# The output projection of half the heads, with 512 columns a matmul and one column of weights

## Chip, cores and metric

The kernel runs on one core of a Trainium2 chip. The metric is the device time of one execution in microseconds (us); the median of several executions is compared.

## What is computed

Two attention layers, A and B, decode one token each, with the same sizes: model width 512, 32 heads of 128, a cache of 8192 keys and values per head, bf16. The two results of 512 numbers are put side by side.

```python
def _A_ref(x, k_cache, v_cache, wq, wo):        # B is the same
    q = (x @ wq) as 32 heads of 128
    scores = jnp.einsum("bhqd,bhkd->bhqk", q, k_cache) * (Dh ** -0.5)
    p = _softmax(scores, axis=-1)
    o = jnp.einsum("bhqk,bhkd->bhqd", p, v_cache)
    return o.reshape(1, 1, 32 * 128) @ wo
...
return jnp.concatenate([a, b], axis=-1)
```

The caches are 256 MiB of the 285 MB that are read; each byte is used once.

## The kernel before

**Tiling.** The 64 heads go in 16 rounds `n` of four (A is rounds 0 to 7, B is 8 to 15). In a round, 32 partitions hold one head, with 256 keys (T) in each partition. `kn` has two buffers for K, `vn` one for V.

**One round.** SyncE (SP) loads K of the next round and V of this one. VectorE (DVE) multiplies K with q in four parts (`plan_mul`, L337). TensorE (PE) folds the 128 products of a key to 8 with identity matmuls of 512 columns (`plan_red`, L346), DVE adds those (`plan_sr`, L357). The maximum is found (`plan_max`, `plan_gmax`: L363, L369, L372) and broadcast with four fp32 matmuls of one row of weights (`plan_exp`, L382); ScalarE (ACT) writes the exponentials to `pt`. In the next round, between its third and fourth fold, PE adds up the sums (`plan_sum`, L399) and multiplies with V in 256 matmuls of four columns (`plan_pv`, L415), and DVE divides (`plan_o`, L424) into `oD`, one column per head, head dimension on partitions.

**wo.** `wo` lies in the K buffer that comes free first (`wo_sb`). A's is loaded whole, B's in pieces of 16, 8, 4, 2, 1 and 1 heads (`WOG`). For a piece of n heads a partition holds n whole rows of wo, one after the other, so `oD` has to be laid out again for pieces of more than one head: `plan_relayout` takes a product with a mask on DVE (L453), a matmul with a selector on PE (L458), and a copy on DVE into `o2` (L462). `plan_wo` (L473) then has wo as weights, 128x128, and one column of `o2` as the moving operand: four matmuls for each of the piece's `j`, which add up in four columns of the bank `qyp`, output columns on partitions. `plan_y` (L481) copies the four columns to `yT`, `plan_out` transposes the eight columns of A and B with one matmul (L485), copies (L488) and stores them with one DMA.

**Order.** Each engine runs a list of instructions written out by hand, in the order in which the plan calls them; a wait stands before the instruction that needs it. All loads are on SP's queue, in order: K of round 15, then A's wo and B's first 16 heads, V of the last round in two pieces (`VLAST`, 192 and 64 of the 256), then the small pieces of B's wo. PE runs rounds 1 to 15 in a loop. The work that follows the last round's scores, A's wo and B's first 16 heads and the layout of B's next two pieces, is a block that PE branches to after round 15 (`cuts[NM][0]` to `[1]`), then it returns to the loop's code for the last `plan_sum` and `plan_pv`, and after that it branches to the last block, with the small pieces and the output. In the program's code the last block stands ahead of the other.

`hrow` [1, 4, 128] fp32 is the constant that `plan_exp` broadcasts with. `rps` has two banks that `plan_red` writes by turns.

Of the kernel before, what the change touches and what calls it, by code (L numbers as in the profile page):

```python
# [8 lines left out]
BF16 = mybir.dt.bfloat16  # L9
F32 = mybir.dt.float32  # L10

P = 128
# [11 lines left out]
class _Plan:  # L24
# [6 lines left out]
    def wait(self, eng, mark):  # L31
        if mark is None:
            return
        ctr, val = mark
        if val <= 0 or self.waited.get((eng, ctr.name), 0) >= val:
            return
        self.waited[(eng, ctr.name)] = val
        self.prog[eng].append((None, ctr, val))

    def op(self, eng, fn, ctr=None, needs=(), inc=1):  # L40

        for m in needs:
            self.wait(eng, m)
        self.prog[eng].append((fn, ctr, inc))
        if ctr is None:
            return None
        ctr.n += inc
        return ctr, ctr.n
# [81 lines left out]
def bass_concat_heads__mha_block_cached__gqa_block_cached__decode_kernel(  # L130
# [18 lines left out]
    NA = 2  # L149
    H, Sk, Dh = ks[0].shape[1:]  # L150
    D = xs[0].shape[2]
    NOUT = wos[0].shape[1]
# [9 lines left out]
    NM = NA * QA  # L162
    NK = 2
    CT = 64
    NCH = T // CT
# [3 lines left out]
    WOG = [[(0, 32)], [(0, 16), (16, 8), (24, 4), (28, 2), (30, 1), (31, 1)]]  # L169
# [4 lines left out]
    with ExitStack() as st:  # L174
# [3 lines left out]
        def sb(name, shape, dt):  # L178
            return ec(nc.sbuf_tensor(name, shape, dt))
# [4 lines left out]
        def flat(ap):  # L184
            return ap.rearrange("p t d -> p (t d)")
# [6 lines left out]
        wo_sb = [flat(kn[:, KW])[:, a * W:(a + 1) * W].rearrange("p (j n) -> p j n", n=NOUT)  # L192
                 for a in range(NA)]
# [6 lines left out]
        ones_f = sb("ones_f", [P, P], F32)  # L200
        ident = sb("ident", [P, P], BF16)
        ident_f = sb("ident_f", [P, P], F32)
        hrow = sb("hrow", [1, G, P], F32)
# [5 lines left out]
        oD = sb("oD", [P, NA, H], BF16)  # L209
        zb = sb("zb", [P, 2, P], BF16)  # L210
        o2 = sb("o2", [P, NA, H], BF16)
        mask = {g: sb("mask%d" % g, [P, P // g], BF16) for g in RG}
        jsel = {g: sb("jsel%d" % g, [P, g], BF16) for g in RG}
        NQ = NOUT // P
        yT = sb("yT", [P, NA, NQ], BF16)
        out_q = sb("out_q", [NA * NQ, P], BF16)

        def ps(name, shape):
            return ec(nc.psum_tensor(name, shape, F32))

        rps = ps("rps", [P, 2, 512])
        acc = ps("acc", [P, 512])
        mtp = ps("mtp", [P, 512])
        bmp = ps("bmp", [P, 512])
        misc = ps("misc", [P, 512])
        qyp = ps("qyp", [P, 512])

        pl = _Plan()
        op, wait = pl.op, pl.wait

        def ctr(name):
            return _Ctr(nc, st, name)
# [6 lines left out]
        s_out = ctr("s_out")  # L239
        c_pool, c_dve, c_act, c_pe = ctr("c_pool"), ctr("c_dve"), ctr("c_act"), ctr("c_pe")  # L240
        c_mul, c_red, c_sr, c_pv = ctr("c_mul"), ctr("c_red"), ctr("c_sr"), ctr("c_pv")

        def dma(eng, dst, src, c, needs=()):
            return op(eng, lambda e: e.dma_start(dst, src), c, needs, inc=16)  # L244


        def const(fn, needs=()):
# [5 lines left out]
            out=ident[:], in_=ones_bf[:], pattern=[[1, P]], compare_op=ALU.is_equal,  # L253
            fill=0.0, base=0, channel_multiplier=-1), [i_onesb])
        i_identf = const(lambda e: e.affine_select(
            out=ident_f[:], in_=ones_f[:], pattern=[[1, P]], compare_op=ALU.is_equal,
# [9 lines left out]
        k_in, v_in, wq_in, wo_in = {}, {}, {}, {}  # L266
        red_done, pv_done, q_done, wo_done = {}, {}, {}, {}
# [25 lines left out]
        for a in range(NA):  # L293
# [6 lines left out]
            m = op("PE", xmm, c_pe, [x_in, i_onesb])  # L300
            x_ready = op("ACT", lambda e, a=a: e.copy(
                xb[:, a].rearrange("p c m -> p (c m)"), (misc if a == 0 else qyp)[:]), c_act, [m])
        misc_free, qy_free = [x_ready], [x_ready]
# [25 lines left out]
        mul_done, sr_done, p_done, m_done, r_done, o_done = {}, {}, {}, {}, {}, {}  # L329
        turn = [None]  # L330

        def nth(n, m=1):
            return slice(n * m, (n + 1) * m) if turn[0] is None else bass.ds((turn[0] * NK + n) * m, m)
# [42 lines left out]
        nb_done = {}  # L376
# [46 lines left out]
        def plan_o(n):  # L423
            o_done[n] = op("DVE", lambda e: e.tensor_tensor(  # L424
                oD[:].rearrange("p a h -> p (a h)")[:, nth(n, G)], acc[:, 0:G],
                rinv[:, nth(n), :].rearrange("p o g -> p (o g)"), ALU.mult),
                c_dve, [pv_done[n], r_done[n]])
# [14 lines left out]
        o2_ready = {}  # L442

        def plan_relayout(*groups):
            assert len(groups) <= 2
            made = []
            for a, g in groups:
                h0, n = WOG[a][g]
                z = z_n[0] % 2
                z_n[0] += 1  # L450
                s = P // n
                zv = zb[:, z, :].rearrange("p (h s) -> p h s", s=s)
                made.append((a, g, h0, n, z, op("DVE", lambda e, a=a, h0=h0, n=n, s=s, zv=zv: e.tensor_tensor(  # L453
                    zv, oD[:, a, h0:h0 + n].unsqueeze(2).broadcast_to([P, n, s]),
                    mask[n][:, None, :].broadcast_to([P, n, s]), ALU.mult),
                    c_dve, [sel_ready[n], o_done[a * QA + (h0 + n - 1) // G], z_free.get(z)])))
            for a, g, h0, n, z, m in made:
                z_free[z] = op("PE", lambda e, n=n, z=z: e.matmul(  # L458
                    z_ps[z][:, 0:n], zb[:, z, :], jsel[n][:], start=True, stop=True),
                    c_pe, [m, z_read[z][0]])  # L460
            for a, g, h0, n, z, m in made:
                o2_ready[a, g] = z_read[z][0] = op("DVE", lambda e, a=a, h0=h0, n=n, z=z: e.tensor_copy(  # L462
                    o2[:, a, h0:h0 + n], z_ps[z][:, 0:n]), c_dve, [z_free[z]])

        def plan_wo(a, g):

            h0, n = WOG[a][g]

            def mm(e):
                r = None  # L470
                for j in range(h0, h0 + n):
                    for i in range(NQ):
                        r = e.matmul(qyp[:, i:i + 1], wo_sb[a][:, j, i * P:(i + 1) * P],  # L473
                                     (o2 if n > 1 else oD)[:, a, j:j + 1], start=(j == 0 and i == 0),
                                     stop=(j == H - 1 and i == NQ - 1), skip_group_check=True)
                return r
            wo_done[a] = op("PE", mm, c_pe, [o2_ready[a, g] if n > 1 else o_done[a * QA + h0 // G],
                                            wo_in[a, g], qy_free[0]])

        def plan_y(a):  # L480
            qy_free[0] = op("DVE", lambda e: e.tensor_copy(yT[:, a, :], qyp[:, 0:NQ]), c_dve,  # L481
                            [wo_done[a]])

        def plan_out():
            m = op("PE", lambda e: e.matmul(bmp[0:NA * NQ, 0:P], yT[:].rearrange("p a q -> p (a q)"),  # L485
                                            ident[:], start=True, stop=True),
                   c_pe, [qy_free[0], nb_done[NM - 1]])
            m = op("DVE", lambda e: e.tensor_copy(out_q[:], bmp[0:NA * NQ, 0:P]), c_dve, [m])  # L488
            done = dma("SP", out[0].rearrange("o (q n) -> (o q) n", q=NA * NQ), out_q[:], s_out, [m])
            wait("SP", done)  # L490


# [50 lines left out]
            load_wo(1, g)  # L543
        z_read[1][0] = gm_done[NM - 1]
        plan_relayout((0, 0), (1, 0))
        plan_wo(0, 0)
        plan_y(0)
        plan_wo(1, 0)
        plan_relayout(*[(1, g) for g in early[BEFORE:]])
        wait("PE", misc_free[0])  # L550
        cuts[NM].append(len(pl.prog["PE"]))
# [2 lines left out]
            plan_pv(NM - 1, t0, t1)  # L554
        cuts[NM].append(len(pl.prog["PE"]))
        plan_o(NM - 1)
        plan_wo(1, BEFORE)
        plan_relayout(*[(1, g) for g in range(len(early), NB) if WOG[1][g][1] > 1])
        for g in range(BEFORE + 1, NB):
            plan_wo(1, g)  # L560
        plan_y(1)
        plan_out()

        for name, at in (("SP", block.sync), ("PE", block.tensor), ("ACT", block.scalar),
# [76 lines left out]
```

## Time and profile before

| | |
|---|---|
| median of 3 runs | 667.73 us (667.52 to 667.88) |
| profiled execution | 668.01 us, of which the span from first to last instruction is 666.28 us |
| mean granted clock of TensorE | 0.756 |
| busy share of the span | PE 66%, DVE 51%, ACT 9%, POOL 0% |
| DMA | 285 MB, 428 GB/s over the span |

Times inside the span are counted from its start. PE is a matmul, PEld the load of its weights, and the two overlap. Matmuls are pipelined, so that the duration of one (165 ns for one of a single column) is not the distance to the next. A granted clock of 1.00 is full, 0.50 half. "issue" marks idle time in which the engine waited for nothing that the profile shows.

### The profile page before, as it was taken

The page shows a single profiled execution, that of the slowest core. Times are in us where ns is not written, and L with a number is a line of the kernel's source. Part 1 is how long each engine was busy: PE and PEld are TensorE (multiplying, and loading weights), DVE is VectorE, ACT ScalarE, POOL GpSimd, SP SyncE. Part 2 cuts the span into 40 slices and gives each one's busy share as a digit, 9 for nine tenths or more (in the row PEclk, how much of TensorE's full clock was granted, in tenths as well). Part 3 has the DMA queues.
Part 4 walks back from the last instruction along what each step waited for, and adds up shares of the span by engine and source line. Part 5 has one row for each costly group of instructions (what it writes and reads, how often), then busy time and mean ns, then how long its engine had stood idle before and what let it go on. Part 6 is the DMA issues. An engine that isn't in the chain of part 4 may idle for free.

```text
span 666.3 us, 12449 instructions
## 1 busy us (share of the span) xinstructions
PE 440.7 (66%) x5646; PEld 252.4 (38%) x5646; DVE 340.2 (51%) x215; ACT 62.4 (9%) x151; POOL 2.8 (0%) x15
## 2 busy tenths in 40 slices
PE   2065875938487594848658484865948486685866
PEld 1022352615244261614425161442626144252645
DVE  1095818356381835638083563809256481925610
ACT  1002002020201002020200202020020202002020
POOL 1000000000000000000000000000000000000000
PEclk9678777769787775978777587877658797765875
DMA  9999999999999999999999999999999999999996
GB/s 378 437 445 438 438 431 433 409 437 441 441 429 433 441 441 425 417 437 441 441 421 441 441 433 429 417 441 441 441 421 441 437 433 429 421 441 441 407 454 274
DMA packets 6076, 285.33 MB, mean 428 GB/s; under 512 B 690, under 2 KB 948, under 8 KB 1204
## 3 DMA queue, kind: packets, MB, share of 16 engines
q1 hardware_dynamic: 6064, 285.22, 99.2%
q8 instruction: 6, 0.10, 0.1%
q14 instruction: 2, 0.02, 0.0%
q10 hardware_dynamic: 4, 0.00, 0.0%
HBM read 285.21 MB, written 0.00 MB: 428 GB/s over the span
## 4 chain that ended last, share of the span: by engine, by line
DMA 62%; PE 25%; DVE 10%; issue 2%; SPq 0%; DVEq 0%; another core or an unknown queue 0%; ACT 0%
DMA kn<-in_B_k_cache_dram 21%; DMA kn<-in_A_k_cache_dram 19%; PE rps L346 15%; DMA vn<-in_A_v_cache_dram 14%; PE acc L415 10%; DVE kn L337 9%; DMA vn<-in_B_v_cache_dram 5%; DMA kn<-in_B_wo_dram 4%; SPq L244 0%; DVE s_sb L357 0%; PE qyp L315 0%; DVEq L117 0%; PE misc L399 0%; ACT qbc L323 0%
## 5 line engine op out<-in xcount | busy, mean ns | idle before, releaser
L346 PE MATMUL rps<-kn,ident 128*128 128x512 bf16 x1024 | 294.5, 456 | 171.7 <-DVE kn L337 171.7
L337 DVE TENSOR_TENSOR kn<-kn,qbc 128x8192 bf16<-128x8192 bf16 x64 | 281.5, 4419 | 98.5 <-DMA kn<-in_A_k_cache_dram 59.0
L346 PEld LDWEIGHTS rps<-kn,ident 128*128 128x128 bf16 x1024 | 112.5, 114 | 340.6 <-issue 266.3
L415 PE MATMUL acc<-pt,vn 128*128 128x4 bf16 x4096 | 108.8, 165 | 5.6 <-DMA vn<-in_B_v_cache_dram 2.4
L415 PEld LDWEIGHTS acc<-pt,vn 128*128 128x128 bf16 x4096 | 108.3, 100 | 6.2 <-DMA vn<-in_B_v_cache_dram 2.7
L357 DVE TENSOR_REDUCE s_sb<-rps 128x64 f32<-128x512 f32 x64 | 44.0, 688 | 110.9 <-PE rps L346 110.9
L394 ACT ACTIVATE pt<-s_sb,negb 32x256 bf16<-32x256 f32 x64 | 54.8, 857 | 2.1 <-ACT negb L386 0.2
L386 ACT ACTIVATE negb<-bmp 128x1 f32<-128x1 f32 x16 | 2.7, 171 | 528.8 <-PE bmp L382 528.8
L424 DVE TENSOR_TENSOR oD<-acc,rinv 128x4 f32 (+1 forms) x16 | 2.6, 163 | 90.9 <-PE acc L415 90.9
L382 PE MATMUL bmp<-gm,hrow 1*128 1x1 f32 x128 | 17.0, 249 | 6.0 <-DVE gm L372 6.0
L382 PEld LDWEIGHTS bmp<-gm,hrow 1*128 1x128 f32 x128 | 15.6, 188 | 10.7 <-DVE gm L372 10.0
L369 PE MATMUL mtp<-ident_f,m 128*1 128x128 f32 x32 | 6.1, 271 | 19.8 <-DVE m L363 19.8
L394 ACT ACTIVATION_READ_ACCUMULATOR pt<-s_sb,negb 32x1 f32 x64 | 15.9, 248 | 0.0
L369 PEld LDWEIGHTS mtp<-ident_f,m 128*1 128x1 f32 x32 | 1.4, 81 | 27.7 <-DVE m L363 27.7
L473 PE MATMUL qyp<-o,kn 128*128 128x1 bf16 x248 | 7.4, 165 | 4.9 <-issue 3.5
L315 PE MATMUL qyp<-vn,xb 128*32 128x512 bf16 x64 | 5.9, 496 | 5.8 <-DMA vn<-in_A_wq_dram 4.3
L473 PEld LDWEIGHTS qyp<-o,kn 128*128 128x128 bf16 x248 | 7.0, 102 | 5.4 <-issue 3.9
L372 DVE TENSOR_REDUCE gm<-mtp 1x4 f32<-1x128 f32 x16 | 4.5, 279 | 7.6 <-PE mtp L369 7.6
L399 PEld LDWEIGHTS misc<-rsum,ones_f 128*128 128x128 f32 x32 | 6.2, 197 | 3.5 <-issue 1.4
L363 DVE TENSOR_REDUCE m<-s_sb 128x1 f32<-128x256 f32 x16 | 6.7, 420 | 0.5
L323 ACT CAST qbc<-qyp 128x512 bf16<-128x512 f32 x4 | 2.3, 586 | 43.0 <-PE qyp L315 43.0
L297 PE MATMUL misc<-ones_bf,kn 1*128 1x128 bf16 x4 | 0.6, 302 | 8.0 <-DMA kn<-in_B_x_dram 8.0
(36 smaller groups left out, 25.1 us busy)
## 6 DMA issues: line engine op xcount, KB each, us to landing
vn<-in_B_v_cache_dram SPq DMA_DIRECT2D x1, 6144.0 KB, 22.2
vn<-in_A_wq_dram SPq DMA_DIRECT2D x1, 4096.0 KB, 12.4
vn<-in_B_wq_dram SPq DMA_DIRECT2D x1, 4096.0 KB, 40.6
kn<-in_A_wo_dram SPq DMA_DIRECT2D x1, 4096.0 KB, 35.1
kn<-in_B_wo_dram SPq DMA_DIRECT2D x1, 2048.0 KB, 39.6
vn<-in_B_v_cache_dram SPq DMA_DIRECT2D x1, 2048.0 KB, 26.7
kn<-in_B_wo_dram SPq DMA_DIRECT2D x1, 1024.0 KB, 28.7
kn<-in_B_wo_dram SPq DMA_DIRECT2D x1, 512.0 KB, 29.5
```

Source lines behind the costliest of these rows:

```text
L315: r = e.matmul(qyp[hh * HP:(hh + 1) * HP, :].rearrange("p (i d) -> p i d", d=Dh), xb[:, a, c, hh * HP:(hh + 1) * HP], w, start=(c == 0), s ...
L337: mul_done[n, c] = op("DVE", lambda e: e.tensor_tensor(k, k, qbc[:, nth(n), :].broadcast_to([P, CT, Dh]), ALU.mult), c_mul, [k_in[n], qbc_ ...
L346: r = e.matmul(rps[:, c % 2, :].rearrange("p (t d) -> p t d", d=DW), ident[:], kn[:, i0, c * CT:(c + 1) * CT, i * DW:(i + 1) * DW], start= ...
L357: sr_done[n, c] = op("DVE", lambda e: e.tensor_reduce(s_sb[:, c * CT:(c + 1) * CT], rps[:, c % 2, :].rearrange("p (t d) -> p t d", d=DW), ...
L363: m_done[n] = op("DVE", lambda e: e.tensor_reduce(m1[:], s_sb[:], AX.X, ALU.max), c_dve, [sr_done[n, NCH - 1]])
L369: m = op("PE", lambda e: e.matmul(mtp[0:1, 0:P], m1[:], ident_f[:], start=True, stop=True), c_pe, [m_done[n], i_identf, gm_done.get(n - 1)])
L372: gm_done[n] = op("DVE", lambda e: e.tensor_reduce(gm[:], mtp[0:1, 0:P].rearrange("o (h p) -> o h p", h=G), AX.X, ALU.max), c_dve, [m, nb_ ...
L382: r = e.matmul(bmp[:, 0:1], hrow[0:1, h, :], gm[0:1, h:h + 1], start=(h == 0), stop=(h == G - 1))
L394: p_done[n] = op("ACT", lambda e, h=h, q=q: e.activation(pt[q, :, h], s_sb[q, :], AF.Exp, bias=negb[q, n:n + 1], scale=scale, accum_out=rs ...
L399: m = op("PE", lambda e: e.matmul(misc[:, 0:G], ones_f[:], rsum[:], start=True, stop=True), c_pe, [p_done[n], misc_free[0]])
L415: r = e.matmul(acc[:, 0:G], vn[:, t, :], pt[:, t, :], start=(t == 0), stop=(t == T - 1))
L473: r = e.matmul(qyp[:, i:i + 1], wo_sb[a][:, j, i * P:(i + 1) * P], (o2 if n > 1 else oD)[:, a, j:j + 1], start=(j == 0 and i == 0), stop=( ...
```

## The change

A's wo and B's first 16 heads change operands: a column of `o2` is the weights (one column), and 512 columns of wo stream past it, so that a `j` needs one matmul instead of four, and the result is a row in one partition: A's in `qyp`, B's in the first bank of `rps`. A's row is copied to bf16 and stored with a DMA of its own. B's is copied to `hrow`, which is no longer needed after the last `plan_exp`, and after the last PV four fp32 matmuls turn it into the four columns of `ycol` (the second bank of `rps`), to which the small pieces then add as before. The last copy, transposition and store have four rows instead of eight.

```diff
-        yT = sb("yT", [P, NA, NQ], BF16)
-        out_q = sb("out_q", [NA * NQ, P], BF16)
+        yT = sb("yT", [P, NQ], BF16)
+        out_a = sb("out_a", [1, NOUT], BF16)
+        yrow = hrow.rearrange("o g p -> o (g p)")
+        out_q = sb("out_q", [NQ, P], BF16)
...
+        yrows, ycol = [qyp, rps[:, 0, :]], rps[:, 1, :]
+
+        def plan_wo_row(a, g, free):
+            h0, n = WOG[a][g]
+            def mm(e):
+                r = None
+                for j in range(h0, h0 + n):
+                    r = e.matmul(yrows[a][0:1, 0:NOUT], o2[:, a, j:j + 1], wo_sb[a][:, j, :],
+                                 start=(j == h0), stop=(j == h0 + n - 1))
+                return r
+            wo_done[a] = op("PE", mm, c_pe, [o2_ready[a, g], wo_in[a, g], free])
+
+        def plan_out_a():
+            m = op("DVE", lambda e: e.tensor_copy(out_a[:], yrows[0][0:1, 0:NOUT]), c_dve, [wo_done[0]])
+            dma("SP", out[0][0:1, 0:NOUT], out_a[:], s_out, [m])
+
+        def plan_yrow():
+            y_ready[0] = op("DVE", lambda e: e.tensor_copy(yrow, yrows[1][0:1, 0:NOUT]), c_dve,
+                            [wo_done[1], nb_done[NM - 1]])
+
+        def plan_ycol():
+            def mm(e):
+                r = None
+                for i in range(NQ):
+                    r = e.matmul(ycol[:, i:i + 1], yrow[0:1, i * P:(i + 1) * P], ones_f[0:1, 0:1],
+                                 start=(i == 0), stop=False, skip_group_check=True)
+                return r
+            op("PE", mm, c_pe, [y_ready[0], sr_done[NM - 1, NCH - 1]])
+
         def plan_wo(a, g):
...
-                        r = e.matmul(qyp[:, i:i + 1], wo_sb[a][:, j, i * P:(i + 1) * P],
-                                     (o2 if n > 1 else oD)[:, a, j:j + 1], start=(j == 0 and i == 0),
+                        r = e.matmul(ycol[:, i:i + 1], wo_sb[a][:, j, i * P:(i + 1) * P],
+                                     (o2 if n > 1 else oD)[:, a, j:j + 1], start=False,
...
-        def plan_y(a):
-            qy_free[0] = op("DVE", lambda e: e.tensor_copy(yT[:, a, :], qyp[:, 0:NQ]), c_dve,
-                            [wo_done[a]])
 
         def plan_out():
-            m = op("PE", lambda e: e.matmul(bmp[0:NA * NQ, 0:P], yT[:].rearrange("p a q -> p (a q)"),
-                                            ident[:], start=True, stop=True),
-                   c_pe, [qy_free[0], nb_done[NM - 1]])
-            m = op("DVE", lambda e: e.tensor_copy(out_q[:], bmp[0:NA * NQ, 0:P]), c_dve, [m])
-            done = dma("SP", out[0].rearrange("o (q n) -> (o q) n", q=NA * NQ), out_q[:], s_out, [m])
+            m = op("DVE", lambda e: e.tensor_copy(yT[:], ycol[:, 0:NQ]), c_dve, [wo_done[1]])
+            m = op("PE", lambda e: e.matmul(bmp[0:NQ, 0:P], yT[:], ident[:], start=True, stop=True),
+                   c_pe, [m, nb_done[NM - 1]])
+            m = op("DVE", lambda e: e.tensor_copy(out_q[:], bmp[0:NQ, 0:P]), c_dve, [m])
+            done = dma("SP", out[0][0:1, NOUT:].rearrange("o (q n) -> (o q) n", q=NQ), out_q[:], s_out, [m])
             wait("SP", done)
...
         plan_relayout((0, 0), (1, 0))
-        plan_wo(0, 0)
-        plan_y(0)
-        plan_wo(1, 0)
+        plan_wo_row(0, 0, qy_free[0])
+        plan_out_a()
+        plan_wo_row(1, 0, sr_done[NM - 1, NCH - 1])
+        plan_yrow()
         plan_relayout(*[(1, g) for g in early[BEFORE:]])
...
         plan_o(NM - 1)
+        plan_ycol()
         plan_wo(1, BEFORE)
...
-        plan_y(1)
         plan_out()
```

## The prediction

> **Bound.** I read the page first, then the chain that ended last, then the timeline of the last 30 us, then windows with their granted clock. The page says that the transfers fill the span:
>
> ```profile
> DMA  9999999999999999999999999999999999999996
> q1 hardware_dynamic: 6064, 285.22, 99.2%
> ```
>
> Work that is added anywhere but at the end is therefore free, as long as it finishes before the next landing. The chain shows where the end is:
>
> ```profile
> 634.11 29.37 DMA kn<-in_B_wo_dram
> 663.49 0.05 issue
> 663.53 0.28 PE qyp L473 x4
> 663.84 0.17 DVE yT L481
> 664.01 0.04 issue
> 664.05 0.28 PE bmp L485
> 664.36 0.28 DVE out_q L488
> ```
>
> The last piece of B's wo lands at 663.49 us, four matmuls use it, and 2.8 us later the program is over. So the time can hardly fall: nothing in the change moves that landing. The question is whether TensorE now comes later than it. The timeline of PE up to there (start, duration, in brackets the idle time before and what ended it):
>
> ```profile
> 638.86 1.05 PE L382 MATMUL bmp<-gm,hrow 1*128 1x1 f32 x8 [0.37 <-DVE gm L372]
> 640.50 2.60 PE L473 MATMUL qyp<-o,kn 128*128 128x1 bf16 x96 [0.27 <-DVE o L462]
> 646.63 1.01 PE L473 MATMUL qyp<-o,kn 128*128 128x1 bf16 x32 [3.53 <-issue]
> 647.99 1.85 PE L473 MATMUL qyp<-o,kn 128*128 128x1 bf16 x64 [0.35 <-DVE yT L481]
> 649.70 0.17 PE L458 MATMUL misc<-jsel,zb 128*128 128x8 bf16 x1
> 651.20 0.58 PE L399 MATMUL misc<-rsum,ones_f 128*128 128x4 f32 x2 [1.31 <-issue]
> 653.58 7.01 PE L415 MATMUL acc<-pt,vn 128*128 128x4 bf16 x256 [1.79 <-DMA vn<-in_B_v_cache_dram]
> 660.97 1.01 PE L473 MATMUL qyp<-o,kn 128*128 128x1 bf16 x32 [0.38 <-DMA kn<-in_B_wo_dram]
> ```
>
> To see there: the 192 small matmuls that the change replaces cost little (26.7 ns each), but a stall of 3.53 us lies in them, in which PE waits for nothing but its own code (in 640 to 660 us the instruction queue q8 moved two packets). After them the last PV pass still waited 1.79 us for the first piece of V. PE has 1.98 us to spare there: the sums of L399 begin at 651.20, PV could follow 0.4 us later, at 651.60, and began at 653.58.
>
> **Term 1.** Removed before PV: 96 + 32 + 64 matmuls, the 3.53 us stall, and the copy of A's columns (L481) with the 0.35 us that PE waited for it. Up to 649.70, where L458 lays out the next heads, all this took 9.2 us.
>
> **Term 2.** Added before PV: 32 + 16 matmuls of 512 columns. The same moving size stands in L346:
>
> ```profile
> 620.99 3.63 PE L346 MATMUL rps<-kn,ident 128*128 128x512 bf16 x16 [1.91 <-DVE kn L337]
> 609.66 0.15 PEld L346 LDWEIGHTS rps<-kn,ident 128*128 128x128 bf16 x1 [0.28 <-issue]
> 610.09 0.15 PEld L346 LDWEIGHTS rps<-kn,ident 128*128 128x128 bf16 x1 [0.28 <-issue]
> ```
>
> At full clock 16 take 3.63 us with the last one's own 0.39 us: (3.63 - 0.39)/15 = 0.216 us each. At half clock they start 0.427 us apart. I take full clock: 48 x 0.216 + 0.17 us for the last to drain = 10.54 us, so the rows end at 651.04. The weight loads (one column) are shorter than L346's and hide under the matmuls, as those do. The two rows write different banks, so B's waits for nothing of A's. The stall should go: in the built program's order the block now holds 2 + 48 + 2 matmuls where before it ran dry after 2 + 96; the block ahead of it grew by only the four of the turn, which L382 shows as eight passes.
>
> **Term 3.** DVE between the rows and the layout of the next heads. The copy of B's row (1x512, from PSUM) waits for the last row matmul, and the two products of L453 stand behind it on DVE; PE's L458 waits for those. Before, they ran under PE's matmuls. The copy lies between 0.28 us (L372, 1x128) and 0.69 us (L357, 128x512); elements per partition set these times, so 0.69. The L453 pair took 0.48 us, starting 0.08 us before the copy ends. With 0.05 and 0.06 us of signalling, L458 starts at 651.04 + 0.05 + 0.69 - 0.08 + 0.48 + 0.06 = 652.24, 2.54 us later than before. Of that 1.98 us is the cover named above; 0.56 us shows: PV runs 654.14 to 661.15 instead of 653.58 to 660.59.
>
> **Term 4.** The turn of B's row, after PV. Four fp32 matmuls with one row of weights, the shape of L382: eight passes, 1.05 us, the last starting 0.80 us after the first. They are queued ahead of all five tail pieces of wo. Branches occupy PE's sequencer until about 0.2 us past PV's end, so the turn starts at +0.27 and the first wo piece at about 0.27 + 0.80 + 0.15 = +1.22 us, where it was +0.38 before: +0.84. Some of it comes back: from that start to the last wo matmul before took 2.83 us, of which about 0.45 us were waits for landings (before 662.99 and 663.53) that a later PE no longer meets. So the last wo matmul ends at 661.15 + 1.22 + 2.38 = 664.75 instead of 663.80: +0.95.
>
> **Term 5.** The rest. A's copy to bf16 (0.69 us) falls at about 647.6, when DVE is idle until the rows end. Its 1 KB store stands on SP, which has nothing to issue after 634.5; it is queued behind loads issued 14 us earlier and ahead of the last store, which is issued at about 665.6, so it costs nothing; if it delayed the end, by less than the final store's own 1.6 us (issue at 664.67, end of span 666.28). The final copy, transposition and store have 4 rows for 8: nothing, or at best 0.1 us.
>
> **Sum.** The profiled execution took 668.01 us (span 666.28 and 1.73 around it). 668.01 + 0.95 = 668.96. The median of the runs is 0.28 below the profiled one, so 668.7 us, +0.14%. A measurement here can tell about 0.2% (1.3 us) from no change.
>
> **Clock.** The granted clock is the large unknown. Columns of the windows: stretch, length, busy us of PE, PEld, DVE, ACT, POOL, then the granted clock.
>
> ```profile
> 618.26:621.68 3.42, 1.51 (x8) 0.53 (x7) 3.42 (x3) 0.00 (x0) 0.00 (x0) 1.00 0.93 402
> 625.09:628.50 3.41, 3.41 (x141) 3.41 (x139) 1.23 (x3) 0.00 (x0) 0.00 (x0) 1.00 1.05 452
> 638.75:642.16 3.41, 2.92 (x76) 2.74 (x77) 0.73 (x5) 2.12 (x6) 0.00 (x0) 1.00 1.00 432
> 642.16:646.63 4.47, 0.94 (x36) 0.86 (x33) 0.00 (x0) 1.50 (x4) 0.00 (x0) 0.50 0.91 389
> ```
>
> In the first stretch PE is busy for only 1.51 us, with 512-column matmuls, and keeps full clock. In the second and third it is busy throughout or nearly, with matmuls of 4 columns or one, and half clock follows. So it is columns streamed that keep the clock, not instructions. The rows stream 512 columns each, but use one of 128 columns of the array. Only L315 has narrow weights here (32 columns), and it runs four side by side. What one column counts for, no row shows. Where the clock's steps of 3.41 us fall differs between executions; if one falls so that the rows begin at half clock for one step, 8 matmuls cost 0.21 us more each (1.7 us), but then the reduction before them had its full clock earlier (10 of its 16 matmuls ran at half here, 2.1 us), so the rows end within about 1.2 us either side of 651.04.
>
> **Rivals.**
> *One column does not keep the clock (slower).* From 642.16 on, 40 of the 48 run at 0.427 us: 642.16 + 17.1 + 0.17 = 659.4, 8.4 us later, and every microsecond past 650.5 delays PV and the end one for one: 677.1, with other places of the steps 675.8 to 677.6. For it: the array is nearly empty. Against it: only streaming has been seen to matter. By the Trainium skill, "TensorE: Matmul & The Clock Gate", Part 1 (The HAM clock gate), the clock depends on how busy PE was in windows of about 3.4 us, and it does not say what a nearly empty array counts as; read plainly it favours full clock, and the steps of 3.41 us here agree with its window. Part 3 (Packing small matmuls) of that page of the Trainium skill warns that with few weight columns most of the array sits idle, which speaks against this form.
> *The rows run faster.* If matmuls of 512 columns with short weight loads overlap, the rows end so early that PV again waits for its landing at 653.58, and only the turn is left: 660.59 + 1.22 + 2.38 = 664.19, +0.4 us, 668.1. The Trainium skill, "TensorE: Matmul & The Clock Gate", section Back-to-back issue gap, gives 131 ns a matmul in a sustained stream of weight loads and 512-column matmuls; by it the rows would end at 647.0. Every full-clock batch of L346 here runs at 216 ns.
> *A code stall stays.* If 3.53 us fall into the new block or its branch, PV is late by that much more: 672.2. The shorter block speaks against it.
>
> **The numbers.** Full clock 0.53, half clock 0.40, faster rows 0.03, stall 0.04. The likeliest has 668.7, its own range 668.1 (short copy, early clock step) to 669.8 (late step); a quarter of it lies above 669.1, the bound of 0.2%. Slower: 0.13 + 0.40 + 0.04 = 0.57. Faster by 0.2% would need the landing at 663.49 itself to move: 0.02. The rest, 0.41, is within. The range must take in most of half clock: 668.0 to 677.4.
>
> **Signs.** Rows 0.216 us apart and no idle "issue" among them; a 1x512 copy of 0.7 us before L453's pair; PV waiting on DVE's chain, not on V; eight passes right after PV; no landing in the last waits. Wrong if rows are 0.43 us apart with a clock of 0.5, if PV still waits for V, or if the chain ends in a landing of wo at 663.5.

## The result and the profile after

The changed kernel takes 669.75 us (median of 12 runs, 668.31 to 672.31) against 667.80 us before (12 runs, 667.52 to 667.94). The ratio of the means is 1.0036, with a 95% interval of 1.0021 to 1.0052 (the medians alone give 1.0029): slower by about 2 us, clear of what can be told from no change. The twelve times do not scatter evenly. Four lie at 668.3 to 668.7, four at 669.6 to 670.5, four at 672.1 to 672.3; the kernel before has nothing like it.

The profiled execution is one of the last group (672.31 us, span 670.5). Its chain that ended last, from the first row matmul on (start, duration, what; times inside the span):

```profile
641.03 9.82 PE qyp L476 x32
650.85 3.47 PE rps L476 x16
654.34 0.68 DVE hrow L486
655.02 0.21 DVE zb L455
...
655.27 0.18 PE misc L460
...
655.87 0.93 issue
656.80 0.54 PE misc L401 x2
657.34 6.84 PE acc L417 x256
664.19 0.26 issue
664.45 1.85 PE rps L496 x8
666.30 0.94 PE rps L509 x32
```

Before, this chain was a landing of 29 us with four matmuls behind it. Now no landing is in it from 641 us on: TensorE and VectorE carry the end by themselves. The rows (L476) take 13.3 us, the copy of B's row (L486) and the layout follow, PV begins at 657.2 instead of 653.6, and the turn (L496) stands alone between PV and the first small piece of wo (L509). The timeline of PE, from the fold of the last round on, shows what is gone (some lines are left out):

```profile
630.95 6.30 PE L348 MATMUL rps<-kn,ident 128*128 128x512 bf16 x16
641.03 9.82 PE L476 MATMUL qyp<-kn,o 128*1 128x512 bf16 x32 [0.27 <-DVE o L464]
650.68 3.62 PE L476 MATMUL rps<-kn,o 128*1 128x512 bf16 x16
656.80 0.54 PE L401 MATMUL misc<-rsum,ones_f 128*128 128x4 f32 x2 [1.14 <-DVE o L464]
657.20 6.99 PE L417 MATMUL acc<-pt,vn 128*128 128x4 bf16 x256
664.45 1.85 PE L496 MATMUL rps<-ones_f,hrow 1*128 1x1 f32 x8 [0.26 <-issue]
666.23 1.01 PE L509 MATMUL rps<-o,kn 128*128 128x1 bf16 x32
667.77 0.35 PE L509 MATMUL rps<-oD,kn 128*128 128x1 bf16 x8
```

There is no bracket "issue" among the rows, so the stall of 3.53 us is gone; there is none "DMA" before PV or L509, so neither V nor wo is waited for. Sixteen rows of B take 3.62 us, as 16 folds do at full clock. A's 32 take 9.82, where the same rate would give 7.1. The windows say why (stretch, length, busy us of PE, PEld, DVE, ACT, POOL, granted clock, then the share and GB/s of the DMA):

```profile
624.17:626.15 1.98, 1.98 (x79) 1.98 (x79) 1.12 (x3) 0.00 (x0) 0.00 (x0) 1.00 1.11 480
626.16:630.90 4.74, 4.74 (x184) 4.74 (x180) 0.00 (x0) 0.00 (x0) 0.00 (x0) 0.50 1.01 436
630.95:636.39 5.44, 5.44 (x17) 1.95 (x14) 0.16 (x1) 0.00 (x0) 0.00 (x0) 0.50 0.97 416
636.40:639.81 3.41, 1.80 (x11) 0.85 (x10) 1.79 (x5) 0.00 (x0) 0.00 (x0) 1.00 1.03 442
639.82:643.22 3.40, 3.13 (x13) 1.53 (x13) 0.27 (x2) 2.49 (x6) 0.00 (x0) 0.50 1.04 448
643.23:646.63 3.40, 3.40 (x10) 1.01 (x9) 0.00 (x0) 1.11 (x4) 0.00 (x0) 0.50 1.03 439
646.65:654.30 7.65, 7.65 (x36) 2.78 (x34) 0.68 (x1) 0.00 (x0) 0.00 (x0) 1.00 0.94 405
664.45:666.23 1.78, 1.78 (x8) 1.76 (x9) 0.26 (x1) 0.00 (x0) 0.00 (x0) 0.50 0.00 0
```

Under PV's four-column matmuls the clock falls to half at 626.16, and it stays there up to 630.90, though PE is busy throughout. The fold of the last round runs at half and gets its full clock at 636.40, with only 0.85 us of it left. In the gap between fold and rows the clock is lost again at 639.81, the rows need until 646.64 to win it back, and the turn at the end is at half once more. The stretch from 643.23 on answers the question that the prediction left open: nothing but matmuls with one column of weights runs in it, and full clock follows. One column does count.

### The profile page after: what moved, and what is told of

It is laid out like the page before. It is cut to its first block, busy times and chain, and to the rows that moved or that the text cites. A ratio compares the mean times of both kernels' runs of the same rounds, so it can differ in the third digit from the quotient of the medians.

```text
span 670.5 us, 12180 instructions
## 1 busy us (share of the span) xinstructions
PE 454.7 (68%) x5510; PEld 255.3 (38%) x5510; DVE 341.4 (51%) x216; ACT 62.4 (9%) x151; POOL 2.8 (0%) x15
## 4 chain that ended last, share of the span: by engine, by line
DMA 55%; PE 32%; DVE 10%; issue 2%; DVEq 0%; another core or an unknown queue 0%; ACT 0%; SPq 0%
DMA kn<-in_B_k_cache_dram 20%; PE rps L348 16%; DMA vn<-in_B_v_cache_dram 14%; PE acc L417 12%; DMA kn<-in_A_k_cache_dram 11%; DVE kn L339 9%; DMA vn<-in_A_v_cache_dram 9%; PE qyp L476 1%; PE rps L476 1%; DVE s_sb L359 0%; PE qyp L317 0%; PE rps L496 0%; PE rps L509 0%; PE bmp L384 0%; DVE m L365 0%
## 5 line engine op out<-in xcount | busy, mean ns | idle before, releaser
L476 PE MATMUL qyp<-kn,o 128*1 128x512 bf16 x32 | 9.8, 483 | 0.3 <-DVE o L464 0.3
```

What stands on the lines that cost most here:

```text
L476: r = e.matmul(yrows[a][0:1, 0:NOUT], o2[:, a, j:j + 1], wo_sb[a][:, j, :], start=(j == h0), stop=(j == h0 + n - 1))
```

## The experiments

All are edits of the changed kernel, except where the kernel before is named; the expectations call experiment 1 e1, and so on. The ratio is to the kernel before, run beside it.

**1. Keep the clock.** PV streams 32 columns of the exponentials instead of 4.

```diff
-        pt = sb("pt", [P, T, G], BF16)
+        VW = 8
+        pt = sb("pt", [P, T + VW, G], BF16)
...
-                    pt[q, :, h], s_sb[q, :], AF.Exp, bias=negb[q, n:n + 1],
+                    pt[q, 0:T, h], s_sb[q, :], AF.Exp, bias=negb[q, n:n + 1],
...
-                    r = e.matmul(acc[:, 0:G], vn[:, t, :], pt[:, t, :],
+                    r = e.matmul(acc[:, 0:VW * G], vn[:, t, :], pt[:, t:t + VW, :].rearrange("p t g -> p (t g)"),
```

> The changed kernel, with each matmul of the PV pass streaming 32 columns of the exponentials instead of 4 (the 28 others add up in columns of the bank that nobody reads). At 26.7 ns a matmul 32 columns still fit, at half clock too, so PV costs the same, but it now streams enough columns to keep TensorE's clock. Theory clock: the twelve times of the changed kernel (668.3 to 672.3 us, in three clusters) spread because the steps of 3.41 us of the clock fall differently, and part of the fold of the last round, of the 48 row matmuls and of the eight passes of the turn runs at half clock. Then the clock stays at 1.00 through the last round's PV and fold, the rows begin earlier, the turn after PV takes 1.0 us instead of 1.85, and the times gather at 668.3 (667.9 to 669.6, the upper ones where one step of half clock still falls between fold and rows). Theory transfers: the spread comes from the landings or from the store of A's row. Then the spread stays at 4 us and the median at 669.7.

Measured: 667.82 us (667.50 to 668.63), ratio 1.0002 (0.9993 to 1.0011). The whole loss and most of the spread are gone. I had expected 668.3, and no less than 667.9; seven of the eleven lie below that. The timeline of PE and windows of this kernel:

```profile
624.06 6.62 PE L418 MATMUL acc<-pt,vn 128*128 128x32 bf16 x256
630.60 3.63 PE L349 MATMUL rps<-kn,ident 128*128 128x512 bf16 x16
637.91 8.37 PE L477 MATMUL qyp<-kn,o 128*1 128x512 bf16 x32 [0.27 <-DVE o L465]
653.19 6.89 PE L418 MATMUL acc<-pt,vn 128*128 128x32 bf16 x256 [0.61 <-DMA vn<-in_B_v_cache_dram]
660.35 1.22 PE L497 MATMUL rps<-ones_f,hrow 1*128 1x1 f32 x8 [0.28 <-issue]
```

```profile
623.60:630.60 7.00, 6.97 (x261) 6.84 (x259) 2.01 (x3) 0.00 (x0) 0.00 (x0) 1.00 1.01 435
630.60:634.23 3.63, 3.63 (x19) 1.48 (x16) 0.16 (x1) 0.00 (x0) 0.00 (x0) 1.00 0.87 370
637.91:646.10 8.19, 8.19 (x32) 2.94 (x33) 0.03 (x1) 3.03 (x8) 0.00 (x0) 0.84 1.08 464
654.23:657.65 3.42, 3.42 (x136) 3.42 (x132) 0.00 (x0) 0.00 (x0) 0.00 (x0) 0.50 0.96 405
657.65:660.08 2.43, 2.42 (x93) 2.30 (x89) 0.00 (x0) 0.00 (x0) 0.00 (x0) 1.00 0.97 395
```

A matmul of 32 columns costs PV what four did, the clock stays at 1.00 through the PV ahead of the last fold and through the fold, the fold takes 3.63 us instead of 6.30, and the rows begin 3.1 us earlier. One stretch at half clock still falls into A's rows (8.37 us, clock 0.84), but now it is covered: PV waits for V again. The last PV, which stands behind a wait, loses the clock for one step all the same, and then its 32 columns win it back (the last two windows). The turn takes 1.22 us for 1.85, in a stretch that mixes both clocks (0.81 in the mean). From the end of PV to the end of the last wo matmul are 3.3 us, for 3.2 in the kernel before, so hardly anything of the turn is left to see; the 668.3 that I expected had more of it. The theory of transfers, which kept the spread, falls.

**2. The same PV in the kernel before**, as a control.

> The kernel before with the same PV of 32 columns, the control of e1. Theory clock: its end hangs on the last landing of wo (663.49 us) and its PV on the landing of V, so a faster TensorE only waits longer: 667.7, at most 0.2 us less from the last transposition at full clock. If wider matmuls cost or gained anything of their own, it would be over 668.2 or under 667.4.

Measured: 667.83 us (667.60 to 668.01), ratio 1.0000 (0.9991 to 1.0009). The profile shows where an earlier TensorE goes:

```profile
649.07 0.59 PE L400 MATMUL misc<-rsum,ones_f 128*128 128x4 f32 x2 [1.31 <-issue]
653.51 6.89 PE L416 MATMUL acc<-pt,vn 128*128 128x32 bf16 x256 [3.85 <-DMA vn<-in_B_v_cache_dram]
```

The sums (L400) come 2.1 us earlier than L399 did, and the wait for V has grown from 1.79 to 3.85 us. So the wider PV gains nothing by itself; in experiment 1 it takes back what the change lost.

**3. A by rows, B by columns.** No copy of B's row, no turn.

```diff
-                                     (o2 if n > 1 else oD)[:, a, j:j + 1], start=False,
+                                     (o2 if n > 1 else oD)[:, a, j:j + 1], start=(j == 0 and i == 0),
...
-        plan_wo_row(1, 0, sr_done[NM - 1, NCH - 1])
-        plan_yrow()
+        wait("PE", sr_done[NM - 1, NCH - 1])
+        plan_wo(1, 0)
...
-        plan_ycol()
```

> The changed kernel with A's wo by rows, but B's first 16 heads by columns as before: no copy of B's row, no turn, final copy and transposition of four columns as in the changed kernel. Theory sum (rows 7 to 10 us, the copy of B's row with the layout behind it 0.9 us, the turn 0.8 to 1.6 us, and what is over the 1.98 us of cover ahead of V shows): the 64 small matmuls cost 1.85 us for the 3.5 of B's rows, PV can follow 651.5 to 655.0 against the landing at 653.5, and nothing stands after PV: 667.7 to 669.2, median 668.2, the upper ones where the rows of A run partly at half clock. Theory that the rows of A alone explain it (B's row and its turn cost nothing that shows): 669.7 with the same spread as the changed kernel.

Measured: 667.67 us (667.53 to 668.00), ratio 0.9999 (0.9990 to 1.0008). Without B's row the loss is gone; A's row alone does not make it:

```profile
640.27 7.07 PE L476 MATMUL qyp<-kn,o 128*1 128x512 bf16 x32 [0.27 <-DVE o L464]
647.27 1.75 PE L509 MATMUL rps<-o,kn 128*128 128x1 bf16 x64
650.49 0.39 PE L401 MATMUL misc<-rsum,ones_f 128*128 128x4 f32 x2 [1.41 <-issue]
653.22 7.01 PE L417 MATMUL acc<-pt,vn 128*128 128x4 bf16 x256 [2.35 <-DMA vn<-in_B_v_cache_dram]
```

A's 32 rows alone leave a wait of 2.35 us for V. But B's row is not enough either: experiment 1 has it and loses nothing. The loss takes both, B's row and the half clock. I had put the upper end at 669.2; even the highest of the eleven stayed under 668.1. What a late clock adds (2.8 us to A's rows in the profile above) would nearly fit into this cover; that any of the eleven had it is not shown, as the one profiled had its rows at full clock.

**4. The layout ahead of the copy.**

```diff
-        plan_yrow()
         plan_relayout(*[(1, g) for g in early[BEFORE:]])
+        plan_yrow()
```

> The changed kernel with the two products of the next layout ahead of the copy of B's row on VectorE, so that they run under the rows and TensorE's layout matmuls follow the rows at once. Theory sum: PV begins about 0.9 us earlier wherever it did not wait for V, the rest stays: median 668.9 (667.9 to 671.4). Rival: the branch and the wait for the copies set PV's begin anyway, or the copy still ahead of the sums holds them: 669.7, no change.

Measured: 669.02 us (668.25 to 671.58), ratio 1.0031 (1.0019 to 1.0044). Two groups, 668.25 to 669.02 and 670.9 to 671.6: the group at 672.2 moved down by 0.5 to 1.4 us, about as the sum has it, while the lowest stayed at 668.3. This rests on matching the groups: the ratio by itself is not clear of the changed kernel's 1.0036. In the profile (668.40 us, one of the lower group) all 48 rows had full clock, and PV waited for V:

```profile
630.95 5.39 PE L348 MATMUL rps<-kn,ident 128*128 128x512 bf16 x16
639.95 7.07 PE L476 MATMUL qyp<-kn,o 128*1 128x512 bf16 x32 [0.27 <-DVE o L464]
646.86 3.62 PE L476 MATMUL rps<-kn,o 128*1 128x512 bf16 x16
653.30 6.98 PE L417 MATMUL acc<-pt,vn 128*128 128x4 bf16 x256 [1.00 <-DMA vn<-in_B_v_cache_dram]
```

```profile
630.95:634.54 3.59, 3.59 (x13) 1.34 (x10) 0.16 (x1) 0.00 (x0) 0.00 (x0) 0.50 0.88 374
634.54:637.95 3.41, 2.17 (x11) 0.67 (x8) 1.11 (x2) 0.00 (x0) 0.00 (x0) 1.00 1.10 471
639.95:650.40 10.45, 10.45 (x48) 3.95 (x48) 1.11 (x4) 3.10 (x8) 0.00 (x0) 1.00 0.99 425
660.54:662.30 1.76, 1.76 (x8) 1.76 (x8) 0.26 (x1) 0.00 (x0) 0.00 (x0) 0.50 0.59 212
```

What is left there is the turn (last line), at half clock.

This profile also shows what parts the groups. Up to the end of the rows PE runs the same instructions as in the changed kernel, and in both profiles the last fold begins at 630.95. Here full clock comes at 634.54, with 1.8 us of the fold left, and stays through the gap; there it came at 636.40, with 0.85 us left, and was lost. Here the rows end at 650.48, there at 654.30: 3.8 us apart, in runs that are 3.9 us apart (668.40 and 672.31).

**5. No turn.** `plan_ycol` is left out, and the first small piece starts the sum; B's first 16 heads are missing from the output.

> The changed kernel without the turn: B's row is still made and copied, but its first 16 heads are left out of the output. Theory sum: the turn is on the path in every execution, because PE reaches it 0.26 us after PV and all pieces of wo stand behind it; it took 1.78 us at half clock in the changed kernel and 1.16 at full clock in e1. Without it 1.2 to 1.8 us go, down to the floor of about 667.6 that the last landing sets: clusters at 667.6, 668.1 and 670.4, median 668.1. Rival (the turn hides behind the wait for wo's landings, and all of the loss stands ahead of PV): 669.7, no change.

Measured: 667.83 us (667.45 to 670.50), ratio 1.0010 (1.0000 to 1.0021). Nine of twelve runs lie at 667.45 to 668.05, three at 670.4 to 670.5. The group that was at 672.2 moved by 1.8 us, which is the turn; the other two, as far as they can be told apart, fell to the floor. So the turn was on the path in all three groups of the changed kernel. Even without it the ratio stays at 1.0010, because of the three late runs. (The 1.16 us that the expectation gives for e1 as full clock is the mixed stretch.)

**6. The turn in bf16.** The row is copied to bf16 (into `xb`, no longer needed) and turned with bf16 ones.

> The changed kernel with B's row copied to bf16 and turned with bf16 matmuls: four passes instead of eight, without fp32 weight loads. Theory: the price of the turn is that of the fp32 weight loads (0.11 us each at full clock, 0.22 at half); four bf16 ones go at the 26.7 ns of the other small matmuls, so the turn shrinks to some 0.2 us: clusters at 667.7, 668.3 and 670.6, median 668.3, within 0.3 us of e5. Rival (a fixed cost of changing weights and bank after PV): less than 0.4 us gained, median over 669.3.

Measured: 667.89 us (667.62 to 670.74), ratio 1.0009 (1.0000 to 1.0018), 0.06 us from experiment 5. Two of the twelve still lie at 670.3 and 670.7, about where the expectation has its late group (670.6). The turn in this profile:

```profile
660.57 0.25 PE L496 MATMUL rps<-ones_bf,xb 1*128 1x1 bf16 x4 [0.26 <-issue]
660.75 1.01 PE L509 MATMUL rps<-o,kn 128*128 128x1 bf16 x32
```

The first wo piece starts 0.18 us after the turn began, where it was 1.78 us (664.45 to 666.23). The price was that of the eight fp32 passes, not of a turn as such. That it lies in their weight loads fits the traces (328 ns a load in the changed kernel, 99 here); the run does not separate the loads from the matmuls.

**7. All three** (1, 4 and 6).

> The changed kernel with the 32-column PV of e1, the layout ahead of the copy of e4, and the bf16 turn of e6. Theory: the rows end near 649.5 whatever the clock's steps, PV waits for V again, the wo pieces wait for their landings again: 667.5 to 667.9 in every execution, the kernel before within 0.2 us, and no faster than e1's fastest, since the last landing is the floor. If it is over 668.3, something of the change is on the path that the sum doesn't have.

Measured: 667.68 us (667.43 to 667.80), ratio 0.9998 (0.9989 to 1.0007). One group is left, and nothing is gained: in the profile it waits for V (0.85 us) and for wo like the kernel before. Its rows end at 650.66, not near 649.5, since part of A's rows still runs at half clock (0.80 in the mean).

**8. Experiment 3 with the PV of experiment 1.**

> A's wo by rows, B's by columns (e3), with the 32-column PV of e1. e3 already reached 667.67 with a spread of 0.5 us, so theory landing: the same 667.6 with the same spread, as nothing of PE is late any more. If the clock still mattered in e3, the median would fall below 667.4.

Measured: 667.68 us (667.58 to 667.77), ratio 0.9999 (0.9990 to 1.0008). The landing is the floor; with the clock out of the way the spread is down to 0.2 us. No version beat the kernel before beyond its interval, so none is put forward.

## Why the prediction was right, and where it missed

*Direction and place: right, the direction in part by luck.* The range held the time, and slower came true. But of the 0.57 for slower 0.40 stood on the rival that one column does not keep the clock, and that is refuted below; the sum itself, 668.7, was within what counts as no change. The same rival made the range wide; the sum's own range ended at 669.8, and six of the twelve runs lie above that, four of them by over 2 us. The bound was read correctly: no version went below about 667.4. The chains of experiments 2, 7 and 8 end in the same landing of wo, at 663.42, 663.20 and 663.17.

*Term 1, the stall: right.* It is gone, and the rows took its place. By itself, in the kernel before, its removal would have gained nothing, because PV waits for V behind it. Experiment 2 shows this for 2.1 us: there the stall is still in (3.54 us), and what PE gains only makes the wait grow to 3.85 us.

*Term 2, the rows: right at full clock, wrong in its spread.* 48 rows take 10.53 us (experiment 4, 639.95 to 650.48) for the 10.54 of the sum. In the profile of the changed kernel they took 13.3 us. The step that failed is the sentence that a late fold and late rows balance, leaving 1.2 us either way. They did not balance: the clock was won back just before the fold ended, lost in the gap, and the rows began at half for 5.6 us. Both paid in the same execution: the rows began 0.5 us later than before (641.03 for 640.50) and took 2.7 us more, so they ended 3.3 us after the 651.04 of the sum. That the clock parts the lowest group from the highest is shown by the two profiles of experiment 4 and the changed kernel. Experiments 1 and 7, which keep the clock through the fold and have a spread of 1.1 and 0.4 us, agree; alone they would not be proof, since their rows also begin earlier and could cover another cause. Which position of the steps makes the middle group was not profiled and is open.

*Term 3: right.* The copy took 0.68 us, and PV began 1.9 us after the layout matmul, as in the sum (652.24 to 654.14). The layout began 0.97 us after the last row instead of 1.2: it starts at 655.27, before the pair of products ends (654.95 + 0.47 = 655.42), so its first matmul does not wait for the second of them.

*Term 4, the turn: right in kind, half its size.* From PV's end to the first wo piece were 2.04 us in the profile after, where the sum has 1.22. The eight passes were priced from L382, which stands right behind the fold and ran at full clock in the row I took; after PV the clock is at half, where they took 1.78 us to the next instruction, for 0.95 in the sum. More came back than the sum allows: from the first wo piece to the end of the last were 1.89 us, for 2.38 in the sum, which left out the wait of 0.21 us before 662.22 in the kernel before. Together, from PV's end to the last wo matmul, 3.93 us stand against 3.60 in the sum and 3.21 before.

So in the profiled run, 4.3 us over the kernel before, 3.6 us are PV's late begin (657.20 for 653.58) and 0.7 us what stands behind PV, where the sum has 0.56 and 0.39. The median (669.75) lies 1.05 over the forecast; it falls into the middle group, so that how much of this is the turn and how much late rows is not shown.

*Term 5: right.* From the last wo matmul to the end of the span were 2.4 us, for 2.5 before, so neither A's store nor the shorter output shows.

*The rival of one column: refuted.* The stretch from 643.23 to 646.63 ended in full clock with nothing else running, and the 48 rows of experiment 4 keep it for 10.45 us. The reading of the Trainium skill, "TensorE: Matmul & The Clock Gate", Part 1 (The HAM clock gate), by which a busy window is enough, held here for the narrow weights. It did not hold for PV with four columns: from 626.16 to 630.90, and in the last PV from 657.20 to 664.19, PE is busy without pause, and the clock stays at 0.50; there the measurement decides.

*The rival of faster rows: refuted.* Full-clock rows stand 0.216 us apart (3.62 us for 16). The 131 ns that the Trainium skill gives in "TensorE: Matmul & The Clock Gate", section Back-to-back issue gap, were not seen.

*A code stall: not seen* in any of the profiles of a changed kernel. The longest "issue" idle of PE behind the last fold is 1.5 us, ahead of the sums, where the kernel before has 1.31. That the 3.53 us before were a wait for code is read from "issue" and the two packets of q8, and no run tested it by itself.

## What to carry to other kernels

Price an instruction from a row that ran at the clock it will have where it is put; the same eight passes took 1.05 us behind the fold and 1.85 behind PV. Work added in front of a landing is free only up to the cover, and the cover has to hold for the slowest position of the clock's steps, not for the one in the profile. Here 256 matmuls of 4 columns lost the clock for what came after them, and widening them to 32 columns, at the same price, kept it for the fold behind them.

## What was not expected of the hardware

A matmul with 4 moving columns and one with 32 took the same time (256 in 6.99 and 6.89 us), but in the PV ahead of the last fold the second kept the granted clock at 1.00 and the first let it fall to 0.50. In the last PV the second even won full clock back, after one step of 3.42 us at half. Weight loads of fp32 with one row took 187 ns at full clock and 328 at half (medians of L382 before and L496 after), so that eight passes went from 1.05 to 1.85 us, although each streams one column.
